# Loading half of the last V tile on four of the sixteen DMA engines

## The chip, the cores and the metric

One core of a Trainium2 chip. The metric is the device time of one execution in microseconds (us), as the median of the runs stated. Kernels can run in a slower state in some executions. Ratios come with a 95% interval. The page numbers, stretches and landings are those of one profiled run of each kernel, whose time is, for the kernel before, 646.39 us.

## The reference

Attention for one query row, 32 heads, 8192 keys, head size 128, bf16, and its gradients:

```python
def _fwd_reference(q, k, v):
    scale = q.shape[-1] ** -0.5
    scores = jnp.einsum('bhqd,bhkd->bhqk', q, k) * scale
    attn = _softmax(scores, axis=-1)
    return jnp.einsum('bhqk,bhkd->bhqd', attn, v)

def reference(q, k, v, grad_out):
    ...
    _out0, _vjp = jax.vjp(_f, q, k, v)      # _f is _fwd_reference
    return (_out0, *[... for _g in _vjp(grad_out)])
```

For each head the kernel reads K and V (2 MB each) and writes dK and dV (2 MB each). That is 268 MB in all. The arithmetic is small beside it.

## The kernel before

Rows of a head are laid out as (p n) d: partition p holds 64 consecutive rows, so 16 KB of contiguous HBM. Loads and stores of whole heads go out on one queue, that of SP. K, V, dK and dV have 3, 2, 2 and 2 buffers.

```python
    def rows_of(x, h, c, parts):
        L = NT // parts
        return x[0, h].rearrange("(p n) d -> p n d", p=P)[:, c * L:(c + 1) * L, :]

    def slots(X, c, parts):
        L = NT // parts
        return X[:, c * L:(c + 1) * L, :]

    def load_v(h):
        Vt[h] = vpool.tile([P, NT, D], BF16, tag="V", name="Vt")
        nc.sync.dma_start(Vt[h][:], rows_of(v, h, 0, 1))

    # ... in outer(), which makes dK and dV a quarter at a time:
        parts = 1
        if h == 0 or h == H - 1:
            parts = 2
        if r % (4 // parts) == 4 // parts - 1:
            c = r // (4 // parts)
            nc.sync.dma_start(rows_of(dst, h, c, parts), slots(G, c, parts))

    # ... in the loop over heads: two heads ahead, after most of the work on V of head h
        outer(h, "dv", 0)
        outer(h, "dv", 1)
        outer(h, "dv", 2)
        if 0 < h and h + 2 < H:
            load_v(h + 2)
        outer(h, "dv", 3)
```

So the dK and dV of the last head (31) are stored in halves, and its V is loaded in one piece.

## Time and profile before

| | before |
|---|---|
| first runs | 646.6 us (646.49 to 646.83, 3 runs) |
| profiled span | 644.6 us |
| DVE, PE, ACT busy | 79%, 77%, 29% |
| queue of SP, share of 16 DMA engines | 98.2% |

The transfers bound this kernel. The interest lies in its last 15 us, where the DMA share falls from 0.93 to 0.06 while no compute engine works. The lines that show it stand in the prediction below. "Landing" always means one of the completion events that each DMA engine leaves for each transfer. I extracted and sorted them from the trace, and they do not name their engine.

### The profile page before, as it was taken

What the parts mean: (1) busy time and instruction counts of PE and PEld (TensorE: products, weight loads), DVE (VectorE), ACT (ScalarE), POOL (GpSimd) and SP (SyncE); (2) the same over time, 40 slices, a digit from 0 to 9 for tenths busy, and PEclk for the clock granted to TensorE, in tenths of its full rate; (3) what the DMA queues carried; (4) which work ended last, traced back from release to release, by engine and by line L of the source; (5) the groups of instructions that cost most, each with busy time, mean ns of one, the idle gap of its engine ahead of it and who ended that gap; (6) DMA issues with size and microseconds to landing.
All of it is one profiled execution on the core that took longest, in us unless ns stands there. A gap on an engine that the chain in (4) does not pass through costs nothing.

```text
span 644.6 us, 20121 instructions
## 1 busy us (share of the span) xinstructions
PE 495.5 (77%) x9242; PEld 432.6 (67%) x9242; DVE 508.7 (79%) x673; ACT 184.3 (29%) x333; POOL 0.7 (0%) x6
## 2 busy tenths in 40 slices
PE   3998888886777977788777788877787787877780
PEld 2886876785676776658665776767586666866670
DVE  5998989877977778877789777797777987778870
ACT  2333333322233231233222332313322133321230
POOL 0000000000000000000000000000000000000000
PEclk9768668765766765686558666666865586665665
DMA  8999999999999999999999999999999999999995
GB/s 349 406 426 432 425 423 428 427 429 427 430 427 429 426 432 424 430 428 425 430 425 430 429 428 427 430 425 429 428 430 426 429 427 430 428 429 428 426 379 213
DMA packets 19833, 269.85 MB, mean 419 GB/s; under 512 B 2397, under 2 KB 2433, under 8 KB 2981
## 3 DMA queue, kind: packets, MB, share of 16 engines
q1 hardware_dynamic: 19701, 268.56, 98.2%
q8 instruction: 72, 1.18, 0.7%
q14 instruction: 12, 0.10, 0.0%
q10 hardware_dynamic: 48, 0.01, 0.0%
HBM read 134.25 MB, written 134.31 MB: 417 GB/s over the span
## 4 chain that ended last, share of the span: by engine, by line
DMA 61%; PE 27%; DVE 7%; ACT 1%; issue 1%; SPq 0%; DVEq 0%; ACTq 0%
DMA Vt<-in_v_dram 60%; PE T_ps L194 15%; DVE XK_sb L152 3%; DVE G_dv L241 3%; PE s_ps L218 3%; PE m_ps L211 2%; PE dp_ps L206 2%; PE s_ps L163 2%; PE dp_ps L211 1%; DMA Kt<-in_k_dram 1%; PE m_ps L328 1%; DVE G_dk L241 1%; ACT XT_sb L185 0%; ACT p_rep L337 0%; PE s_ps L179 0%
## 5 line engine op out<-in xcount | busy, mean ns | idle before, releaser
L194 PE MATMUL T_ps<-ident_f,Vt 128*128 128x128 f32 x1024 | 209.5, 373 | 26.1 <-DMA Vt<-in_v_dram 24.4
L194 PEld LDWEIGHTS T_ps<-ident_f,Vt 128*128 128x128 f32 x1024 | 176.1, 201 | 44.8 <-PE m_ps L316 26.7
L241 DVE TENSOR_TENSOR G_dv<-p_rep,qd 128x2048 bf16<-128x2048 bf16 x128 | 148.2, 1220 | 58.8 <-DMA out_dram<-G_dv 48.2
L241 DVE TENSOR_TENSOR G_dk<-ds_rep,qd 128x2048 bf16<-128x2048 bf16 x128 | 155.7, 1219 | 1.6 <-DMA out_dram<-G_dk 0.5
L185 ACT COPY XT_sb<-T_ps 128x1024 f32<-128x1024 f32 x128 | 128.3, 1007 | 91.6 <-PE T_ps L194 88.0
L152 DVE STREAM_TRANSPOSE XK_sb<-Kt 128x1024 f32<-128x1024 f32 x128 | 149.3, 1217 | 6.2 <-DMA Kt<-in_k_dram 5.7
L163 PE MATMUL s_ps<-q_blk,XK_sb 128*128 128x4 bf16 x2048 | 59.6, 168 | 75.3 <-DVE pdt L265 68.2
L163 PEld LDWEIGHTS <-XK_sb 128*128 128x128 bf16 x2048 | 56.9, 104 | 82.7 <-DVE pdt L265 75.4
L206 PE MATMUL dp_ps<-do_blk,XT_sb 128*128 128x2 bf16 x2048 | 66.5, 164 | 19.7 <-ACT XT_sb L185 19.7
L206 PEld LDWEIGHTS <-XT_sb 128*128 128x128 bf16 x2048 | 63.7, 101 | 26.4 <-ACT XT_sb L185 22.4
L211 PE MATMUL dp_ps<-ds_rep,Kt 128*128 128x1 bf16 x2048 | 64.0, 165 | 0.0
L211 PEld LDWEIGHTS <-Kt 128*128 128x128 bf16 x2048 | 59.5, 104 | 5.4 <-issue 5.3
L275 ACT COPY dq_all<-dp_ps 128x1 f32<-128x1 f32 x32 | 5.1, 159 | 193.2 <-PE dp_ps L211 186.3
L211 PEld LDWEIGHTS <-Vt 128*128 128x128 bf16 x1472 | 41.3, 97 | 0.6
L211 PE MATMUL m_ps<-p_rep,Vt 128*128 128x1 bf16 x1472 | 40.8, 164 | 0.0
L218 PE MATMUL s_ps<-Vt,p_rep 128*4 128x512 bf16 x144 | 36.4, 398 | 0.0
L337 ACT ACTIVATE p_rep<-e,rinv 128x256 bf16<-128x256 f32 x32 | 16.3, 509 | 63.3 <-DVE rinv L335 63.3
L335 DVE RECIPROCAL rinv<-m_ps 128x1 f32<-128x1 f32 x32 | 5.4, 168 | 33.8 <-PE m_ps L328 33.7
L218 PEld LDWEIGHTS <-p_rep 128*4 128x4 bf16 x144 | 11.2, 87 | 20.1 <-issue 6.0
L260 ACT CAST qd<-s_ps 128x256 bf16<-128x256 f32 x32 | 11.9, 372 | 31.0 <-PE s_ps L256 31.0
L327 ACT ACTIVATE e<-s_ps,nbias 128x64 f32<-128x64 f32 x32 | 10.0, 314 | 32.2 <-DVE nbias L323 32.2
L169 DVE TENSOR_TENSOR sm<-s_ps,in_quad 128x256 f32<-128x256 f32 x32 | 13.6, 425 | 6.5 <-PE s_ps L163 3.6
(56 smaller groups left out, 191.4 us busy)
## 6 DMA issues: line engine op xcount, KB each, us to landing
Vt<-in_v_dram SPq DMA_DIRECT2D x32, 2048.0 KB
Kt<-in_k_dram SPq DMA_DIRECT2D x31, 2048.0 KB
out_dram<-G_dv SPq DMA_DIRECT2D x30, 2048.0 KB
out_dram<-G_dk SPq DMA_DIRECT2D x30, 2048.0 KB
out_dram<-G_dv SPq DMA_DIRECT2D x4, 1024.0 KB
out_dram<-G_dk SPq DMA_DIRECT2D x4, 1024.0 KB
Kt<-in_k_dram SPq DMA_DIRECT2D x4, 512.0 KB
scratch<-four SPq DMA_DIRECT2D x9, 8.0 KB
```

The source lines that it names most:

```text
L152: nc.vector.transpose(XK[h][:, :, :, u, :], slots(Kt[h], u, NCH).rearrange("p g d -> p (g d)").bitcast(F32).rearrange("p (g w j) -> p g w ...
L163: nc.tensor.matmul(out[:, g, :], lhsT=cols[:, g, c // 2, c % 2], rhs=q_blk[:, h, c, :], start=(c == 0), stop=(c == 2 * NB - 1), skip_group ...
L169: nc.vector.tensor_tensor(x["sm"][:], x["s"][:, 0:NT].rearrange("p (a g) -> p a g", a=NQ).unsqueeze(2) .to_broadcast([P, NQ, NCH, CH]), in ...
L185: nc.scalar.copy(X[:], st[h].pop("T")[:])
L194: nc.tensor.transpose(T_ps[:, i, :], words[:, m * P:(m + 1) * P], ident_f[:])
L206: nc.tensor.matmul(st[h]["dp"][:, n:n + 2], lhsT=X[:, i, e2, :], rhs=do_blk[:, h, e2, :], start=(e2 == 0), stop=(e2 == 1), skip_group_chec ...
L211: nc.tensor.matmul(out_col, lhsT=Xt[:, n, :], rhs=rep[:, n, 0:1], start=(n == 0), stop=(n == NT - 1), skip_group_check=True)
L218: nc.tensor.matmul(x["s"][0:R, :], lhsT=x["p"][:, R * g:R * (g + 1), 0], rhs=Vt[h][:, R * g:R * (g + 1), :].rearrange("p n d -> p (n d)"), ...
L241: nc.vector.tensor_tensor(slots(G, r, 4).rearrange("p n (a b) -> p n a b", b=R), slots(rep, r, 4).unsqueeze(2).to_broadcast([P, Q, D // R, ...
L260: nc.scalar.copy(x["qd"][:].rearrange("p a d -> p (a d)"), x["s"][:, 256:512])
L327: nc.scalar.activation(e[:], x["sn"], ACT.Exp, bias=nbias[:], scale=scale, accum_out=rs[:])
L337: nc.scalar.activation(x["p"][:], e[:].unsqueeze(2).to_broadcast([P, NT, R]), ACT.Copy, scale=rinv[:])
```

## The change

Seven of the sixteen DMA engines are ahead of the rest when the last V loads. The intent is to give them the second half of that V, and so to take work off the late ones. A transfer of 128 partitions goes to all sixteen. Cut as 124 + 4 partitions, it should go to the first four; the prediction gives the source.

```diff
     def load_v(h):
         Vt[h] = vpool.tile([P, NT, D], BF16, tag="V", name="Vt")
-        nc.sync.dma_start(Vt[h][:], rows_of(v, h, 0, 1))
+        if h < H - 1:
+            nc.sync.dma_start(Vt[h][:], rows_of(v, h, 0, 1))
+        else:
+
+            nc.sync.dma_start(slots(Vt[h], 0, 2), rows_of(v, h, 0, 2))
+            for lo, hi in ((0, P - 4), (P - 4, P)):
+                nc.sync.dma_start(slots(Vt[h], 1, 2)[lo:hi], rows_of(v, h, 1, 2)[lo:hi])
```

## The prediction

> **What bounds the kernel now.** I read the page first: which resource is full, and where it stops being full.
>
> ```profile
> PE 495.5 (77%) x9242; PEld 432.6 (67%) x9242; DVE 508.7 (79%) x673; ACT 184.3 (29%) x333; POOL 0.7 (0%) x6
> ...
> DMA  8999999999999999999999999999999999999995
> GB/s 349 406 426 432 425 423 428 427 429 427 430 427 429 426 432 424 430 428 425 430 425 430 429 428 427 430 425 429 428 430 426 429 427 430 428 429 428 426 379 213
> ...
> q1 hardware_dynamic: 19701, 268.56, 98.2%
> q8 instruction: 72, 1.18, 0.7%
> ```
>
> No compute engine passes 79%, the DMA engines are at 9 tenths in 38 slices, and one queue fills 98.2% of them. So the transfers bound the kernel. But the last two slices (16.1 us each) fall to 379 and 213 GB/s. The stretches of the tail, with DMA share and GB/s in the last two columns:
>
> ```profile
> 621.00:633.00 12.00, 4.80 (x108) 4.22 (x106) 7.59 (x9) 2.29 (x7) 0.00 (x0) 0.51 0.93 389
> 633.00:639.00 6.00, 0.00 (x0) 0.00 (x0) 0.00 (x0) 0.00 (x0) 0.00 (x0) 0.50 0.57 241
> 639.00:641.00 2.00, 0.00 (x0) 0.00 (x0) 0.00 (x0) 0.00 (x0) 0.00 (x0) 0.50 0.21 84
> 641.00:643.00 2.00, 0.00 (x0) 0.00 (x0) 0.00 (x0) 0.00 (x0) 0.00 (x0) 0.50 0.06 25
> ```
>
> From 633 nothing computes, and the share is 0.57 = 9 of 16 engines, then 0.21, then 0.06 = 1 of 16. So the DMA engines do not finish together: seven are done by 633, one works alone to 643. The timeline shows the last big stores being issued long before:
>
> ```profile
> 620.23 2.61 SPq L251 DMA_DIRECT2D out_dram<-G_dv  x2
> 625.05 0.33 SPq L284 DMA_DIRECT2D out_dram<-fin_sb  x1
> 626.68 2.60 SPq L251 DMA_DIRECT2D out_dram<-G_dk  x2
> ```
>
> The last piece of dK is issued by 629.3, 14 us before the end: compute is not what ends the kernel, the backlog of the slowest DMA engine is. The page's chain of waits follows instructions and does not show this; I trust the stretches.
>
> To see each engine I sorted the 16 completion events that each transfer leaves in the trace (one per DMA engine). Numbers are us, my extraction:
>
> ```
> V of head 31      598.12 598.37 598.61 598.64 598.90 600.59 603.64 | 609.05 609.19 609.46 610.36 610.61 610.96 611.16 611.55 | 612.73
> last half of dK   632.89 632.91 632.92 632.96 632.97 633.06 633.67 | 639.59 639.66 639.79 639.85 640.12 640.23 640.38 640.77 | 643.38
> dK of head 25     534.90 535.16 535.35 535.41 535.61 537.33 540.34 | 544.44 ...                                      546.87 | 548.44
> head 26's scratch (4 partitions, queued right behind it)  535.53 535.80 537.51 540.53
> ```
>
> Seven engines lead, eight follow, one is last (call it L). L is never idle: its landings of consecutive 2 MB transfers are 602.85, 607.85, 612.73, 617.75, about 4.9 us each, to the end. Its lag fits the 72 instruction fetches of q8 (about 1 us each), which fall unevenly; that reading is inferred.
>
> **What the skill says.** (1) The Trainium skill, "DMA: Bandwidth & Descriptors", section "Why a DMA increments its semaphore by 16 and not by 1": a DMA issued by SP uses the largest k up to 16 that divides the slowest dimension, on the lowest-numbered k engines. 124 = 4 x 31 and 4 both give k = 4. The trace agrees for 4 partitions: a scratch store left four engine completions and one immediate one. No run shows 124 yet. (2) Same page, "Queues, rings and completion order": each DMA engine takes its ring in order, so what is taken off L's ring moves everything behind it forward. The trace agrees: each scratch completion comes 0.17 to 0.19 us behind the dK completion of one engine. (3) Same page, "Rules for kernel authors": two transfers to disjoint partition halves are not worth it, since both spray over all 16 engines. Here the premise fails on purpose.
>
> The scratch row also says **which engines the first four are**: they trail 535.35, 535.61, 537.33 and 540.34. So all four are among the seven leaders, and one (call it F, 603.64 for the last V) is the slowest leader. L is not among them.
>
> **The change part by part.**
> - *First half of V, 128 partitions, 8 KB each.* Each engine gets 8 packets of 8 KB instead of 8 of 16 KB. Packets of 16 KB took 611 ns at the median and 8 KB ones 309 ns, so nothing is lost per byte. L's V takes half of 612.73 - 607.85 = 4.88, that is 2.44. **L gains 2.44 us**, as do the other eleven engines outside the first four.
> - *Second half.* 31 + 1 packets of 8 KB on each of the first four, instead of 8 per engine of all 16: 24 more, at about 0.306 us from start to start in the tail, is **+7.34 us on each of four engines**. F then has V at 603.64 - 2.44 + 32 x 0.306 = 611.0.
> - *The end by engine.* L: 643.38 - 2.44 = 640.94. The eight: at most 640.77 - 2.44 = 638.3. F: it takes 633.67 - 603.64 = 30.03 us from V to the end now, which is six 2 MB transfers at 4.86 plus small ones, so it has no idle time to absorb the delay: 633.67 + 7.34 = 641.01. The other three have V by 606 to 608 and some idle time before later stores, so they end below 638.4. The end is the later of L and F, 641.0: **2.4 us sooner**.
> - *V's arrival.* It was complete at 612.73; now the first half lands at 610.3 (L) and the second at 611.0 (F). In the compiled order the first two groups of transposes wait for the first load alone and the third for the other two; in the trace the third began 4 us after the first. So compute starts about 2.4 us sooner. That is worth nothing by itself, since L is fed anyway.
> - *Two more issues on SP.* Each takes about 0.33 us. The eight completion semaphores rotate, and a DMA waits for the one eight before it. With two more, head 29's dV store waits for head 27's dK, which lands at 588.08, instead of going at 582.94; head 29's dK store goes at about 598 instead of 594.08. All rings still hold V then (598 at the earliest), so this is hidden.
>
> Sum: 646.6 - 2.4 = 644.2. I add 0.3 because the end is the maximum of two engines that tie within 0.1 us, and any disturbance of F can only delay it: **644.5 us**.
>
> **The rivals.**
> - *F becomes the bound.* Its 8 KB loads may run slower than 8 KB stores (none is in this trace), or an extra instruction fetch falls on it. At 0.34 us per packet F ends 1.1 later, and the time is 645.3. If each packet took twice as long (destinations of one engine collide with another's), F ends 9.8 us later: 654. For: F has no slack. Against: 16 KB loads and stores land at the same spacing.
> - *The transfer goes to one engine, or to all.* One engine with 1 MB would need 128 x 0.306 = 39 us and delay the end by 20 us or more; all 16 would leave 646.6 or a little above. Against both: the rule for k and the scratch stores.
> - *The semaphore rotation starves the leaders.* A late dV store would matter only if a ring ran dry on L; its ring is over 20 us deep. No effect.
> - *Compute had been the end.* An earlier V would then give 1 to 2 us. Against: 14 us from last issue to end.
>
> **Range and chances.** Three runs of before span 0.34 us, so noise is small. The gain cannot exceed L's 2.44 by much: low 643.8. If F's packets are slow or a fetch hits F, it shrinks: high 646.0. A gain of 2% would need 13 us; a loss of 2% needs the packet-doubling or one-engine rival. Faster 0.005, within 2% 0.975, slower 0.02.
>
> **What the profile will show.** Right: the first half of V leaves 16 engine completions, the other two 4 each; L's last completion near 640.9; the fourth of the first four near 641.0, V complete near 611; the share after 633 nearer 0.8 than 0.57; the 0.06 stretch gone. Wrong if: 124 partitions leave other than 4 completions; V's second half lands well after 612; or the last completion belongs to one of the first four by more than 1 us over L.

## The result, and the profile after

The changed kernel took 646.54 us (645.53 to 647.31, 4 runs), the kernel before 646.72 (646.49 to 647.59, 4 runs). The ratio is 0.9994 [0.9977, 1.0011]. A ratio is the mean time of one kernel's fast runs over that of the other's of the same rounds, so it is not quite the ratio of the medians. A second session with more rounds (e11 below) gave 0.9995 [0.9981, 1.0008]. The predicted gain of 2.1 us is not there, and the time lies outside the predicted range of 643.8 to 646.0.

The tail of the changed kernel, in the same stretches as before. The columns are the stretch and its length (us), the busy time of PE, PEld, DVE, ACT and POOL with counts, the granted PE clock, the DMA share and GB/s:

```profile
621.00:633.00 12.00, 5.05 (x107) 4.43 (x105) 8.58 (x10) 2.29 (x7) 0.00 (x0) 0.50 0.96 402
633.00:639.00 6.00, 0.00 (x0) 0.00 (x0) 0.00 (x0) 0.00 (x0) 0.00 (x0) 0.50 0.79 331
639.00:641.00 2.00, 0.00 (x0) 0.00 (x0) 0.00 (x0) 0.00 (x0) 0.00 (x0) 0.50 0.14 58
641.00:643.00 2.00, 0.00 (x0) 0.00 (x0) 0.00 (x0) 0.00 (x0) 0.00 (x0) 0.50 0.09 37
```

From 633 to 639 the share is 0.79 and no longer 0.57, as foretold. So the load was moved. But the last stretch did not empty: 0.09 of sixteen is one to two engines still at work after 641. The page's row by slices (40 slices of 16.1 us) tells where the balance was paid for. Slice 38 is 596.5 to 612.7:

```profile
GB/s 336 421 424 428 429 422 429 427 426 428 429 428 428 427 429 427 427 429 429 428 425 431 424 430 427 433 423 431 425 431 425 428 427 426 431 429 426 372 397 242
```

The kernel before had 426 to 428 GB/s in slices 37 and 38 and then 379; here slice 38 has 372. The first slow slice now comes while V loads, with the DMA engines still at 9 tenths. The stretch 606 to 621, before and then after, shows it:

```profile
606.00:621.00 15.00, 12.53 (x263) 11.72 (x264) 11.14 (x17) 4.15 (x8) 0.00 (x0) 0.61 0.93 395
606.00:621.00 15.00, 12.07 (x263) 11.53 (x264) 11.53 (x17) 4.16 (x8) 0.00 (x0) 0.61 0.93 369
```

At the same share of 0.93 the rate fell from 395 to 369 GB/s. The engines were as busy and moved less.

The landings after (us), second row for the two pieces of the second half:

```
V of head 31, first half          595.49 595.69 595.82 595.99 596.58 599.06 601.39 | 608.44 608.76 609.07 609.50 609.69 609.83 610.17 611.01 | 611.19
second half, 124 then 4           608.40 608.93 610.00 613.54, then 608.75 609.25 610.31 613.85
last half of dK                   633.77 633.79 633.87 | 638.02 ... 639.90 | 642.20  643.87
```

The two pieces left four engine completions each, so the engine count was right. The engine that ends at 642.20 is L, traced backwards transfer by transfer. The one at 643.87 is F, the slowest of the first four: its landings run 613.85, 618.74, 623.65, 628.48, 634.12, 636.55, 638.99, 641.44, 643.87: 4.8 to 4.9 us for each 2 MB, once 5.64, then 2.4 for each megabyte, so F was busy to the end. L gained 1.18 us instead of 2.44, and F is the new end.

The issues on SP's queue from 580 to 605, before and after (start, duration, queue, line, transfer):

```profile
582.51 0.33 SPq L80 DMA_DIRECT2D Vt<-in_v_dram  x1
582.94 0.42 SPq L251 DMA_DIRECT2D out_dram<-G_dv  x1
583.41 0.91 SPq L368 DMA_DIRECT2D blocks<-scratch  x1
594.08 0.35 SPq L251 DMA_DIRECT2D out_dram<-G_dk  x1
602.69 0.33 SPq L251 DMA_DIRECT2D out_dram<-G_dv  x1
```

```profile
581.84 0.33 SPq L84 DMA_DIRECT2D Vt<-in_v_dram  x1
582.23 1.28 SPq L86 DMA_DIRECT2D Vt<-in_v_dram  x2
588.25 0.37 SPq L257 DMA_DIRECT2D out_dram<-G_dv  x1
593.07 0.93 SPq L374 DMA_DIRECT2D blocks<-scratch  x1
598.14 0.38 SPq L257 DMA_DIRECT2D out_dram<-G_dk  x1
604.29 0.33 SPq L257 DMA_DIRECT2D out_dram<-G_dv  x1
```

The dV store went from 582.94 to 588.25 and the dK store to 598.14, as predicted from the rotation of the completion semaphores (588.08 and about 598). The late engines still had V in front of these stores.

The long piece of the chain of waits that ended last, before and then after (start, us, what):

```profile
582.51 30.21 DMA Vt<-in_v_dram
```

```profile
588.25 30.49 DMA out_dram<-G_dv
...
618.83 4.63 DVE G_dv L247 x4
```

Before, compute waited for V until 612.7. After, the last dV waits until 618.74 for a buffer: the store of head 29's dV on F, queued behind F's share of V. Before, the last dV began at 617.85, and after at 618.83. So the earlier first half of V bought compute nothing, but that does not set the end either.

### The profile page after: what moved, and what is told of

Its sections match the earlier page's. It is cut to its first block, busy times and chain, and to the rows that moved or that the text cites. A ratio compares the mean times of both kernels' runs of the same rounds, so it can differ in the third digit from the quotient of the medians.

```text
span 644.9 us, 20124 instructions
## 1 busy us (share of the span) xinstructions
PE 494.9 (77%) x9242; PEld 431.5 (67%) x9242; DVE 508.7 (79%) x673; ACT 184.1 (29%) x333; POOL 0.7 (0%) x6
## 3 DMA queue, kind: packets, MB, share of 16 engines
q8 instruction: 72, 1.18, 0.7%
## 4 chain that ended last, share of the span: by engine, by line
DMA 61%; PE 24%; DVE 10%; ACT 1%; issue 1%; SPq 0%; DVEq 0%; ACTq 0%
DMA Vt<-in_v_dram 41%; DMA Kt<-in_k_dram 15%; PE T_ps L200 11%; DVE XK_sb L158 6%; DMA out_dram<-G_dv 5%; DVE G_dv L247 4%; PE s_ps L224 3%; PE s_ps L169 3%; PE dp_ps L217 2%; PE dp_ps L212 2%; PE m_ps L217 1%; DVE G_dk L247 1%; PE s_ps L185 1%; PE m_ps L334 1%; PE m_ps L322 0%
```

## The experiments

**Theory after the first look.** F had V at 613.85 instead of 611.0, because its 32 packets of 8 KB took 12.46 us, 0.389 us each instead of 0.306. From then on it behaved as predicted: 643.87 - 613.85 = 30.02 us, against the 30.03 of the prediction. Of the 256 load packets of 8 KB between 590 and 614, 73 took over 450 ns. The normal one takes 309. **Theory A**: a DMA engine slows when it works on SBUF partitions that another engine is working on. In a 128-partition transfer each engine has its own eight partitions (source below, with e4); the 124-partition one spreads four engines over nearly all of them. **Rivals**: B, half-row loads are slow by themselves; C, the two halves of the same HBM rows collide; D and H, a megabyte on four engines is slow whatever its partitions.

### Which engines lead: p1_probes

```diff
         if 0 < h and h + 2 < H:
+            if h in (22, 24, 25, 27):
+                n = 5 + (22, 24, 25, 27).index(h)
+                nc.sync.dma_start(probe[n - 5, 0:n], ident[0:n, :])
             load_v(h + 2)
```

> No theory is at stake: the kernel before with four tiny stores of 5, 6, 7 and 8 partitions behind the loads of four late heads, to tell which numbers the leading DMA engines and the last one have. The last one should show up first in one of the stores of 5 to 8 partitions, or only in the 9-partition load; time within 0.5 us of before.

One run, 646.22 us. Each tiny store lands about 0.18 us behind the transfer ahead of it on the same engine. The 5-partition store left completions at 457.49, 457.57, 459.00, 461.54 and 469.18, and the transfer ahead ended at 468.99. So, with engines counted from 0 as in the prediction's source, **the last engine, L, is DMA engine 4**. The 8-partition store left 554.63, 554.97, 555.07, 556.42, 559.76, then 565.62, 565.81, 568.34. The 7-partition store had no fifth leader, so engine 7 leads too, and 5 and 6 are late.

### The split alone: e1_halves_all16

```diff
-        nc.sync.dma_start(Vt[h][:], rows_of(v, h, 0, 1))
+        parts = 2 if h == H - 1 else 1
+        for c in range(parts):
+            nc.sync.dma_start(slots(Vt[h], c, parts), rows_of(v, h, c, parts))
```

> The last head's V in two halves, each of 128 partitions, so both on all 16 DMA engines: the split alone, without the redirect. Theory A (the slow packets of the changed kernel come from DMA engines 0 to 3 writing partitions that others are writing at the same time): 8 KB load packets keep 0.31 us, each half takes 2.4 to 2.5 us on every engine, time as before, 646.3 to 647.2 us. Theory B (8 KB load packets with a 16 KB pitch in HBM are slow by themselves once many engines read them): packets of 0.5 to 0.6 us also here, V of the last head 2 to 4 us later on most engines, time 648 to 650 us.

646.80 us (646.18 to 647.00, 4 runs), ratio 1.0000 [0.9984, 1.0015]. All 256 load packets of 8 KB took 309.6 ns in the mean, none over 320. B falls: splitting a load costs nothing, and half rows are not slow.

### Another source: e2_other_source

Wrong results on purpose.

```diff
-                nc.sync.dma_start(slots(Vt[h], 1, 2)[lo:hi], rows_of(v, h, 1, 2)[lo:hi])
+                nc.sync.dma_start(slots(Vt[h], 1, 2)[lo:hi], v[0, 0].rearrange("(x p n) d -> x p n d", x=2, p=P)[0][lo:hi])
```

> Wrong results on purpose: as the changed kernel, but the second half of the last V is read from a contiguous megabyte of another head's V (8 KB pitch instead of 16 KB), the destinations and the engines unchanged. Theory A (collision at the destination): packets of 0.5 to 0.6 us stay, the slowest of the first four engines has its 32 packets in 12 to 12.5 us and the second half complete near 613.9, time 646 to 647 us. Theory C (collision at the source in HBM, both halves of the same 16 KB rows being read at once): packets fall to 0.31 us, 32 of them in 9.8 to 10 us, complete near 611, time 644.2 to 645.2 us.

646.24 us (645.96 to 646.55, 4 runs), ratio 0.9993 [0.9979, 1.0007]. Of the 256 packets 69 took over 450 ns, against 73 in the changed kernel, with the same mean (392 and 391 ns). F's 32 packets took 11.1 us, less than the 12 to 12.5 foretold for A. C falls: it is not the rows in HBM.

### A store instead of a load: e3_store_redirect

V in one load as before. The last megabyte of dK goes to the first four engines:

```diff
-            nc.sync.dma_start(rows_of(dst, h, c, parts), slots(G, c, parts))
+            cuts = (0, P)
+            if h == H - 1 and which == "dk" and c == 1:
+                cuts = (0, P - 4, P)
+            for lo, hi in zip(cuts, cuts[1:]):
+                nc.sync.dma_start(rows_of(dst, h, c, parts)[lo:hi], slots(G, c, parts)[lo:hi])
```

> V in one load as before; instead the very last megabyte stored (second half of the last head's dK) goes as 124 + 4 partitions on DMA engines 0 to 3. Nothing loads then. Theory A or C (the slow packets are special to a load that meets other loads): store packets keep 0.31 us, 32 of them 9.8 to 10 us after the first half's landing near 631.2, so the last completion on those four is near 641.1 to 641.5, the slowest other engine 2.4 us sooner than before (near 641), time 644.2 to 645.2 us. Theory D (any transfer whose partitions are spread over four engines meets other traffic and slows to 0.39 us): 32 packets take 12.5 us, last completion near 643.8, time 646.5 to 647 us.

647.58 us (647.49 to 647.86, 5 runs), ratio 1.0014 [1.0002, 1.0027], slower than both expectations. Stores slow as well: the four ended at 642.50, 643.84, 644.27 and 644.51, and packets of up to 1361 ns occur. The theory as first put ("a load that meets loads") was too narrow. What remained was A with reads of SBUF included, or D: four engines with a megabyte are slow whatever they touch.

### Own or foreign partitions: e4_store_own and e5_store_foreign

This pair decides. The same four engines write the same megabyte of HBM; only the SBUF partitions that they read differ (rows are repeated, so results are wrong):

```diff
+            if h == H - 1 and which == "dk" and c == 1:
+                out = rows_of(dst, h, c, parts).rearrange("(e j r) n d -> j e r (n d)", e=4, j=4)
+                for j, p0 in enumerate((0, 1, 32, 33)):          # e5: (16, 17, 48, 49)
+                    nc.sync.dma_start(out[j], slots(G, c, parts)[p0:p0 + 16:4].rearrange("p n d -> p (n d)").unsqueeze(1)
+                                      .to_broadcast([4, 8, NT // 2 * D]))
+            else:
+                nc.sync.dma_start(rows_of(dst, h, c, parts), slots(G, c, parts))
```

Which partitions are whose comes from the Trainium skill, "DMA: Bandwidth & Descriptors", section "The descriptor swizzle": engine = 8 * (partition >> 6) + ((partition >> 2) & 7). That gives 0 to 15 and 32 to 47 for engines 0 to 3, and 16 to 31 and 48 to 63 for engines 4 to 7. The trace does not name engines, so it does not show the formula directly; the pair agrees with it.

> Wrong results on purpose. As the redirected last store (1 MB on DMA engines 0 to 3, the same rows of HBM), but each of the four reads only partitions that are its own in a 128-partition transfer (0 to 15 and 32 to 47, rows repeated). Theory A (an engine slows when it works on partitions that another engine is working on, on the SBUF side): no packet over 450 ns on the four, 32 packets in 9.8 to 10 us, last completions on the four 640.4 to 641.2, time 644.2 to 645.0 us. Rival H (the collisions are in HBM, or come from four engines carrying a megabyte): the same slow packets as in the redirected store, last completions 642 to 644.3, time 646.5 to 647.8 us.

> Wrong results on purpose. The same four stores to the same rows of HBM, but read from partitions 16 to 31 and 48 to 63, which in a 128-partition transfer belong to DMA engines 4 to 7, all four of them late ones and engine 4 the last of all. Theory A: each pair shares its partitions for as long as both work, packets of about 0.6 us on both sides, the last completion 6 to 14 us later than with own partitions, time 650 to 658 us. Rival H: the same as with own partitions, within 1 us.

Own: 643.92 us (643.81 to 644.02, 4 runs), ratio 0.9958 [0.9942, 0.9973]. Foreign: 651.59 us (651.37 to 651.65, 4 runs), ratio 1.0075 [1.0059, 1.0090]. The tails, first own, then foreign:

```profile
633.00:639.00 6.00, 0.00 (x0) 0.00 (x0) 0.00 (x0) 0.00 (x0) 0.00 (x0) 0.50 0.68 284
639.00:641.00 2.00, 0.00 (x0) 0.00 (x0) 0.00 (x0) 0.00 (x0) 0.00 (x0) 0.50 0.17 71
641.00:643.00 2.00, 0.00 (x0) 0.00 (x0) 0.00 (x0) 0.00 (x0) 0.00 (x0) 0.50 0.00 0
```

```profile
633.00:639.00 6.00, 0.00 (x0) 0.00 (x0) 0.00 (x0) 0.00 (x0) 0.00 (x0) 0.50 0.70 227
639.00:641.00 2.00, 0.00 (x0) 0.00 (x0) 0.00 (x0) 0.00 (x0) 0.00 (x0) 0.50 0.30 91
641.00:645.00 4.00, 0.00 (x0) 0.00 (x0) 0.00 (x0) 0.00 (x0) 0.00 (x0) 0.50 0.25 78
```

Divide GB/s by share x 16. From 639 to 641, own gives 71 / 2.7 = 26 GB/s per busy engine, foreign 91 / 4.8 = 19, and from 641 to 645 foreign gives 78 / 4.0 = 20. From 630 on, own has 336 packets of 8 KB, none over 332 ns; foreign has 336 too, 86 of them over 450 ns. D and H fall: four engines can carry a megabyte at full speed if they keep to their own partitions. With own partitions the gain is the 2.4 us that the prediction wanted: the four engines end at 640.5 to 640.8 and L at 641.0, where it was 643.4. This is a bound and not a way to a right kernel, because the rows that L is to be relieved of lie in L's partitions, and another engine must go there to move them.

The foreign case has a detail that checks the reading. I had expected all four pairs to suffer, but the first quarter landed at 633.42, 635.49, 635.57 and 636.02: one of the four was not slowed. Engine 7, the owner of one set, is a leader and had little left to store. My expectation called it late; the probe run says otherwise. And of the nine late engines just three, as many as were visited (4, 5 and 6), had the first half of the last dK later: 639.63, 640.01 and 646.60, where with own partitions the nine landed from 637.06 to 638.40 and at 640.96.

### The same for loads: e6_load_own and e7_load_foreign

256 KB of extra loads ahead of the last V, into a side buffer; right results:

```diff
+        if h == H - 1:
+            src = rows_of(v, h, 1, 2).rearrange("(e j r) n d -> j e r (n d)", e=4, j=16)
+            for j, p0 in enumerate((0, 1, 32, 33)):              # e7: (16, 17, 48, 49)
+                nc.sync.dma_start(side[p0:p0 + 16:4], src[j])
         nc.sync.dma_start(Vt[h][:], rows_of(v, h, 0, 1))
```

> Right results. The last V in one load, and ahead of it 256 KB of extra loads on DMA engines 0 to 3 into partitions that are theirs (32 packets of 8 KB in all). Theory A: none of the 32 over 450 ns, mean 309 to 320 ns. Rival H: mean 340 to 400 ns, as in the changed kernel while the slow engines load. Time within 1 us of before.

> Right results. The same extra loads from the same rows of HBM, but into the partitions of DMA engines 4 to 7, which load K at that time. Theory A: a third or more of the 32 packets at 550 to 700 ns, and 16 KB packets of the engines they meet stretched as well. Rival H: as with own partitions. Time within 2 us of before.

One run each, 646.34 and 647.04 us. Own: all 32 packets at 309 ns. Foreign: the 16 packets that started before 595.7 took 309 ns; of the 16 after that, 14 took 506 to 653 ns. Of the 16 KB packets in 590 to 605, 43 of 322 took over 900 ns, against 5 of 364 with own partitions. So partitions decide for loads too, which is what the change does, and a foreign partition is not slow by itself: half of the visiting packets took 309 ns.

But in one point A is too narrow for loads: engines that nobody visits pay as well. All nine late engines got head 31's K at 601.63 to 603.50, against 599.52 to 602.83 with own partitions, though only three of them (4, 5, 6) were visited. Of the 20 packets of 16 KB that started from 598.2 to 599.4 none took under 769 ns; with own partitions all 30 took 611 to 619. This rests on one run of each.

### What it cost L

Under A, L should suffer while the redirected writes cross its partitions. The time from head 28's dV to head 31's K on the last engine says so: 4.91 us before (597.94 to 602.85) and 4.89 in e1, but 6.16 in the changed kernel (598.07 to 604.23), 6.22 in e2 and 6.42 in e11. Part of this came back at once: the next transfer, head 28's dK, took 4.47 instead of 5.00. Over both the cost is 0.5 to 0.9 us (9.91 before and 9.95 in e1; 10.63, 10.48 and 10.84 in the changed kernel, e2 and e11). L ended 1.18 us sooner where 2.44 was foretold, so it fell 1.26 short; what makes up the rest is not settled. I show this as a pattern over runs; no run isolates L alone.

### Smaller doses: e8_store_half, e9_store_3quarters, e10_load_quarter

e8 and e9 leave the first 16 or 8 of the 32 row slots of the last dK megabyte on all engines (`keep`) and redirect the rest:

```diff
+            out, src = rows_of(dst, h, c, parts), slots(G, c, parts)
+            if h == H - 1 and which == "dk" and c == 1:
+                nc.sync.dma_start(out[:, 0:keep], src[:, 0:keep])
+                for lo, hi in ((0, P - 4), (P - 4, P)):
+                    nc.sync.dma_start(out[lo:hi, keep:], src[lo:hi, keep:])
+            else:
+                nc.sync.dma_start(out, src)
```

e10 is the change with a cut at three quarters of V instead of a half.

> The store redirect at half the dose: of the last megabyte of dK only the second half of each row (4 KB per partition) goes as 124 + 4 partitions on DMA engines 0 to 3. Theory A: the last engine loses 1.2 us of work and ends near 642.2, the four have 32 packets of 4 KB, some of them slowed, and end by 640; time 645.2 to 645.8 us (0.8 to 1.5 us faster than before). If slowing on the four or on the last engine ate it at any dose: 646.5 us or more.

> Three quarters of the last megabyte of dK (6 KB per partition) on DMA engines 0 to 3. Theory A: the last engine ends near 641.6; the four need 32 packets of 6 KB, 7.4 us without slow packets and 9 to 10 us with the share of slow ones of the full redirect, so they end at 640.5 to 642; time 644.6 to 645.6 us.

> The change at half its dose: the last quarter of each row of the last V (4 KB per partition) instead of the last half on DMA engines 0 to 3. Theory A: the last engine gains 1.2 us and loses some 0.6 us where its own K load meets the redirected writes; the slowest of the four is 2 to 4 us clear of the end; time 645.8 to 646.5 us, at best 0.9 us faster than before.

| run | time, us | ratio to before |
|---|---|---|
| e8, half of the store | 645.28 (644.79 to 645.45, 5 runs) | 0.9979 [0.9966, 0.9991] |
| e9, three quarters | 645.39 (644.97 to 645.68, 5 runs) | 0.9982 [0.9969, 0.9994] |
| e3, all of it | 647.58 (647.49 to 647.86, 5 runs) | 1.0014 [1.0002, 1.0027] |
| e10, a quarter of V | 646.62 (646.48 to 646.68, 5 runs) | 1.0001 [0.9988, 1.0013] |

The tail of e8:

```profile
633.00:639.00 6.00, 0.00 (x0) 0.00 (x0) 0.00 (x0) 0.00 (x0) 0.00 (x0) 0.50 0.74 288
639.00:641.00 2.00, 0.00 (x0) 0.00 (x0) 0.00 (x0) 0.00 (x0) 0.00 (x0) 0.50 0.08 31
641.00:643.00 2.00, 0.00 (x0) 0.00 (x0) 0.00 (x0) 0.00 (x0) 0.00 (x0) 0.50 0.01 2
```

At half the dose the four end by 639.2, slow packets included (37 of 256 packets of 4 KB took at least 1.45 times the median), and L ends at 641.7. **e8 is a right version that beats both kernels**, by 0.2%. Redirecting a load is worse than redirecting a store at the same dose: e10, just outside its expected 645.8 to 646.5, gained nothing. There the way to head 31's K took L 6.5 us (597.92 to 604.39), which ate all of the 1.2 us that it was relieved of.

### The change again: e11_after_again

> The changed kernel again, for a second profile and a tighter interval. Theory A: 32 packets of the slowest of the four again take 11.5 to 13 us and it ends last or within 1 us of the last engine, time 646.0 to 647.0 us.

646.62 us (645.36 to 647.09, 5 runs). In its profile F's 32 packets took 11.44 us (602.48 to 613.92), 69 of 256 packets were over 450 ns, F ended at 643.94 and L at 642.18. The expected 11.5 us at least for the four was missed by a hair, but F had all of V no earlier (613.92, and 613.85 in the first profile); the rest is as expected.

### What stays open

How two engines share is not settled. In e5 both sides run at about half speed; in e7 all loading engines slow. In e3 some packets took 1069 to 1361 ns, which could be three or four parties on one set of partitions, but packets carry no address. Between 605 and 608 of the changed kernel nearly all loading engines were slow at once (51 of 64 packets of 8 KB starting then took over 450 ns), more than four visitors can meet one by one. The stores of those 3 us, 27 packets of 16 KB, were hardly touched: 2 took over 700 ns, where 611 is normal. So there loads slowed loads and not stores. No run tests whether the direction of a transfer decides. The runs show that partitions decide, not by which port or bank.

## Why the prediction was wrong

- **Which bound, which engines.** Right. The end is the backlog of the slowest DMA engine; 124 + 4 partitions go to four engines; they are four leaders. The share from 633 to 639 rose to 0.79. One reading was loose: after 617.75 L's transfers took 5.59 and 5.37 us (to 623.34 and 628.71), not about 4.9 to the end. The sum does not use it, because it starts from L's measured end.
- **First half of V.** Right in itself: in e1 all halves cost half. For L it landed 2.49 us after the transfer ahead instead of 4.88, but the prediction missed that L would also pay: in the end L was 1.18 us sooner and not 2.44.
- **Second half of V.** This is the step that failed: "24 more, at about 0.306 us from start to start in the tail, is +7.34 us on each of four engines". The term was mis-sized for F: 32 packets cost it 12.46 us, not 9.8. The spacing came from transfers in which every engine kept to its own partitions, and I applied it to engines that left theirs.
- **The end by engine.** The form was right, the later of L and F. The measured terms are L 642.20 for 640.94 and F 643.87 for 641.01; before, the end was 643.38. So F alone cost the whole gain; with F on time, L's own landing would have left 1.2 us of it.
- **The rivals.** "F becomes the bound" is what happened, by its own bracketed reason, "destinations of one engine collide with another's". The argument against it, that 16 KB loads and stores land at the same spacing, did not bear on it. It deserved more than the tail of the chances.
- **Issue order and semaphores.** Right, and hidden.
- **Range.** Its upper end of 646.0 lies 1.5 us above the forecast, which is 0.05 us more for each of F's 32 packets; the measured 0.083 lies beyond.

## What to carry to other kernels

When the end is a queue's backlog, look at the landing of each DMA engine before balancing bytes between them: the mean share hides both the leaders and the last one. Balancing by partition counts that use fewer engines moves those engines onto partitions that others are using, and both sides may then run at half speed (among loads even engines that nobody visits, in e7); count that in, do it with a store near the end rather than with a load amid loads, and take less than the arithmetic of bytes allows.

## What the Trainium skill lacked or had wrong

- "SBUF — State Buffer", section "SBUF: two separate sides", names a likely cause, which I did not look up: several DMA engines that write may contend on the AXI ports, by which DMA reaches SBUF. It speaks of writes alone, while e5 shows reads too (86 of 336 store packets over 450 ns, none with own partitions). Its section "Who interferes with whom" says that only the port pair shared by DVE and GpSimd contends. Taken at its word this leaves out DMA against DMA, which e7 shows (506 to 653 ns instead of 309, with the same compute as in e6, where none was slow).
- "DMA: Bandwidth & Descriptors", section "Why a DMA increments its semaphore by 16 and not by 1", paragraph "How many engines (k)": the rule held (124 partitions left four completions). It does not say that a small k makes engines leave their own partitions, nor what that costs: 0.36 to 0.39 us per 8 KB packet on F instead of 0.306.
- No page says that the sixteen engines drift apart in a long kernel: 14.6 us between first and last at the last V. "DMA: Bandwidth & Descriptors", section "Latency and other measured facts", has engines 7 and 15 as usually the slower ones and guesses at a cause in transfers issued by GpSimd, of which this kernel has none; here engine 7 leads and engine 4 is last (p1). The 72 instruction fetches, if they fall unevenly, are a possible reason, not a shown one.
